# Queries x state in batches 0 to 3 by halves of TensorE's array, a second product for batch 1, a written order

## The chip, the core and the metric

The kernel runs on one core of a Trainium2 chip. The metric is the device time of one execution in microseconds (us), the median of the runs shown. Five engines work side by side, each with its own stream of instructions: PE (TensorE: matmuls, with PEld for its weight loads), DVE (VectorE), ACT (ScalarE), POOL (GpSimd) and SP (SyncE, which issues most transfers). They wait for each other by semaphores. SBUF is the working memory, PSUM (8 banks of 128 x 512 fp32) takes what PE writes.

## What is computed

Eight batches, eight heads, 576 positions, head size 64; linear attention with a norm, then a Fourier mixing and a feed-forward network (FFN):

```
kv  = einsum('bhsd,bhse->bhde', k, v)          # the state, 64 x 64 a head
out = einsum('bhsd,bhde->bhse', q, kv)         # queries x state
rms = sqrt(mean(out * out, axis=-1) + 1e-06)
x   = out / rms * g_norm                       # [8, 576, 512] after a transpose
u   = x + real(fft(fft(x, axis=1), axis=2))
un  = (u - mean(u)) / sqrt(var(u) + 1e-06)     # over the last axis
y   = u + relu(un @ w_ch1) @ w_ch2             # 512 -> 2048 -> 512
```

## The kernel before, in words

The attention, the Fourier mixing and a part of the FFN (the "early FFN", three of its sixteen slices of the hidden layer) are laid out as 1699 operations, each a Python closure that emits a handful of instructions of one engine. `Plan.run` (L443) lays them in an order: it walks through a time line with the costs that each operation was given, and on each engine takes the ready operation of the lowest rank whose buffers are free. The instructions emitted in the first 300 us of that time line are then tied to this order engine by engine (`pin`, L417). The ranks come from the batch and the stage (`rank`, L789), shifted by the table `SHIFT` (L55), one value for a stage, an engine and a rank, 275 in all. Behind the planned part the rest of the FFN follows (L1804 to L2338), most of it tied to the order in which it is written.

A batch goes through these stages. `plan_kv` (L919) forms the state on PE (L963, 64x64 quarters of the array) and copies it to SBUF on ACT (L988); for batch 0 DVE also writes a state scaled by g_norm (L998). `plan_q` (L1043) turns the queries on PE (L1055), and ACT copies them to `fq` (L1059). The 288 rows of a half of the sequence are three tiles of 96 rows (the first has 98), t = 0, 1, 2. `plan_out` (L1069) multiplies queries by state on PE (L1083), one PSUM bank for the even heads and one for the odd. A pair of heads lies on the partitions of one `fq` column block, 64 rows for each head; the weights are the queries, cut into 64 and 34 columns, so that each matmul uses one 64x64 quarter of the array: 2 sides x 4 pairs x 2 heads x 2 parts = 32 matmuls a product, which the trace shows as 64 records (each fp32 matmul here is two). Then ACT squares the product in PSUM (L1115), DVE sums the squares (L1120), and the product goes to `x`: in batch 0 a second product with the scaled state is made and ACT copies it (L1100); in batch 1 (`GAIN_AT_ONCE`) DVE copies it and multiplies by g_norm in one instruction (L1104); in batches 2 to 7 ACT copies it and POOL multiplies (L1133).

`plan_y` (L1140) makes 1/rms. `plan_fold` (L1176) multiplies `x` by it on DVE, one instruction a side (L1188), sums four columns for the zeroth frequency (L1193), and folds `x` (L1200). `plan_split` and `plan_folds` split it in two parts on POOL and ACT (L1217 to L1293), `plan_seq` (L1298, L1317) and `plan_chn` (L1352, L1361) are the two Fourier stages, and their result is added to `x` on DVE for batch 0 and on POOL for the others (L1400, L1403). `plan_turn` (L1434) turns `x` on PE (L1459) and splits it into `unTh` and `unTl`. When a block of 512 tokens is turned, `plan_early` (L1544) runs the early FFN on it (L735, L753). `plan_w` (L1481) converts the weights, mostly on DVE (L671 to L680, L700, L1509), for PE's means L694.

PE also gets fillers that compute nothing that is used (L809, `plan_spare`): 30 at once, 40 and 22 more when 12 and 38 us of the planned time have passed, ranked behind all other work of PE.

Of the kernel before, what the change touches and what calls it, by code (L numbers as in the profile page):

```python
# [9 lines left out]
F32 = mybir.dt.float32  # L10
# [4 lines left out]
ALU = mybir.AluOpType  # L15
# [12 lines left out]
NA = 3  # L28
# [26 lines left out]
SHIFT = {  # L55
    ("", "DVE", -100): -32718,
    ("", "DVE", 85): 3,
    ("", "HOST", 0): 2612.5,
    ("", "HOST", 9000): 2922.5,
    ("", "PE", 85): 147129,  # L60
    ("", "POOL", 20): 10887.5,
    ("", "POOL", 40): 273026.5,
    ("", "POOL", 50): 16174,
    ("", "POOL", 60): 1017789,
    ("", "POOL", 70): 281483.5,
    ("", "SP DMA", -40): -314778,
    ("", "SP DMA", 10): -20802,
    ("", "SP DMA", 20): 72028,
    ("", "SP DMA", 85): 2143.5,
    ("chn", "ACT", -34): 1891,  # L70
    ("chn", "ACT", 16): 4142,
    ("chn", "ACT", 26): 116005,
    ("chn", "ACT", 36): 50922.5,
    ("chn", "ACT", 46): -188.5,
    ("chn", "ACT", 56): 2260,
    ("chn", "ACT", 66): 110596,
    ("chn", "ACT", 76): 8930,
    ("chn", "DVE", -34): -62060.5,
    ("chn", "DVE", 16): 5303,
    ("chn", "DVE", 26): 368,  # L80
    ("chn", "DVE", 36): -19935,
    ("chn", "DVE", 46): -922,
    ("chn", "DVE", 56): -4020.5,
    ("chn", "DVE", 66): 21267,
    ("chn", "DVE", 76): -121.5,
    ("chn", "PE", -34): -28856,
    ("chn", "PE", 16): -65422,
    ("chn", "PE", 26): 521738.5,
    ("chn", "PE", 36): 17419.5,
    ("chn", "PE", 46): 5106,  # L90
    ("chn", "PE", 56): 518354.5,
    ("chn", "PE", 66): 62546,
    ("chn", "PE", 76): 6630.5,
    ("chn", "POOL", 16): 32868,
    ("chn", "POOL", 26): -43448,
    ("chn", "POOL", 36): -41076.5,
    ("chn", "POOL", 46): -6341.5,
    ("chn", "POOL", 56): -10643,
    ("chn", "POOL", 66): -356,
    ("chn", "POOL", 76): -2168,  # L100
    ("chn", "SP DMA", -34): -17259.5,
    ("chn", "SP DMA", 16): -1294,
    ("chn", "SP DMA", 26): -16518,
    ("chn", "SP DMA", 36): -290.5,
    ("chn", "SP DMA", 46): 17435,
    ("chn", "SP DMA", 56): 26457.5,
    ("chn", "SP DMA", 66): 16.5,
    ("chn", "SP DMA", 76): 7747,
    ("dft", "POOL", -37): 2039.5,
    ("dft", "SP DMA", -37): -192772.5,  # L110
    ("dft_d", "ACT", -35): 391,
    ("dft_d", "DVE", -35): -3433,
    ("dft_d", "POOL", -35): -9543.5,
    ("dft_d", "SP DMA", -35): -202629,
    ("dft_split", "ACT", -37): -41818.5,
    ("dft_split", "ACT", 9): 22267,
    ("dft_split", "POOL", -37): 19163,
    ("dft_split", "POOL", 9): -3864.5,
    ("early", "ACT", -100): -72646,
    ("early", "DVE", -100): 3540,  # L120
    ("early", "PE", 1000): 112,
    ("early", "PE", 1010): 57509,
    ("early", "PE", 1020): 41715.5,
    ("early", "PE", 1030): 133598,
    ("early", "PE", 1040): 42048.5,
    ("early", "PE", 1060): -1666,
    ("early", "PE", 1070): -100,
    ("early", "PE", 1080): 6247.5,
    ("early", "SP DMA", -100): 11271,
    ("fold", "DVE", -36): 29687.5,  # L130
    ("fold", "DVE", 14): 44762,
    ("fold", "DVE", 24): 13,
    ("fold", "DVE", 34): 4778,
    ("fold", "DVE", 44): 21,
    ("fold", "DVE", 54): -6924.5,
    ("fold", "DVE", 64): 4500,
    ("fold", "DVE", 74): -6233.5,
    ("folds", "ACT", 14): 10045,
    ("folds", "ACT", 24): -1988,
    ("folds", "ACT", 34): 110076,  # L140
    ("folds", "ACT", 44): 5822,
    ("folds", "ACT", 54): 23702.5,
    ("folds", "ACT", 64): -8652.5,
    ("folds", "ACT", 74): 1672,
    ("folds", "POOL", 14): 32875,
    ("folds", "POOL", 24): 8206,
    ("folds", "POOL", 34): 4127.5,
    ("folds", "POOL", 44): -47893.5,
    ("folds", "POOL", 54): 14868.5,
    ("folds", "POOL", 64): 7840,  # L150
    ("folds", "POOL", 74): 114,
    ("kv", "ACT DMA", -40): -329,
    ("kv", "ACT", -40): 1747,
    ("kv", "ACT", 10): -2622,
    ("kv", "ACT", 40): 1206,
    ("kv", "ACT", 50): 3461.5,
    ("kv", "ACT", 60): 6444.5,
    ("kv", "DVE", -40): -5070.5,
    ("kv", "PE", -40): -58409.5,
    ("kv", "PE", 10): -1672,  # L160
    ("kv", "PE", 20): -4880,
    ("kv", "PE", 30): -524.5,
# [12 lines left out]
    ("out", "ACT", -58): 1017.5,
# [2244 lines left out]
```

## Time and profile before

| | |
|---|---|
| median of 3 runs | 953.65 us (953.2 to 955.07) |
| profiled execution, its own time | 954.79 us |
| its span, first to last instruction | 953.0 us |
| busy in the span | PE 936.5, PEld 783.8, DVE 682.8, ACT 387.5, POOL 443.9 us |
| mean granted clock of PE | 0.998 of full speed |

The span is shorter than the time by what lies before the first and behind the last instruction, 1.8 us. Busy time of PE is the union of its matmuls, whose ends are modelled: a short gap between two small matmuls can hide in it, so the time that a product takes is read from where the next work starts. "Issue" as the end of an idle time means that the engine waited for nothing that the profile shows. The clock is given as a share of 2.4 GHz, at 0.50 it is 1.2 GHz.

### The profile page before, as it was taken

Reading aid. Unit: us, or ns where it says so; the run is one execution under the profiler, and the core shown is the slowest. Engines: PE = TensorE matmul, PEld = TensorE weight load, DVE = VectorE, ACT = ScalarE, POOL = GpSimd, SP = SyncE. Lnnn points to the kernel's source line nnn. Section 1 sums busy time; section 2 is a strip of 40 time slices with the busy share of each in tenths; the row PEclk is TensorE's granted clock in tenths of the full one; section 3 lists DMA queues with packets and bytes.
Section 4 is the critical chain, followed back from the end, with each engine's and each line's share of the span. In section 5 each row is a group of like instructions: output and inputs, shape, how many; then the busy total and the mean of one; then the engine's idle time right before and its main releaser. Section 6 shows DMA issues by size and latency. Waiting matters only on the chain.

```text
span 953.0 us, 18483 instructions
## 1 busy us (share of the span) xinstructions
PE 936.5 (98%) x7182; PEld 783.8 (82%) x7182; DVE 682.8 (72%) x1202; ACT 387.5 (41%) x743; POOL 443.9 (47%) x440
## 2 busy tenths in 40 slices
PE   9898999999999999999999999999999999999998
PEld 7787988888888877888888888888888888888886
DVE  5798787857948689999367876596658685674554
ACT  3666877778545323533314322342225212521110
POOL 3576787786644235656715053724462437210000
PEclk9999999999999999999999999999999999999999
DMA  8899587735456698988497496429543774213412
GB/s 271 229 288 313 163 285 233 255 98 195 166 204 247 235 384 325 371 300 291 176 379 304 146 341 253 173 76 332 200 154 111 254 280 181 81 76 140 182 55 88
DMA packets 108566, 210.53 MB, mean 221 GB/s; under 512 B 45292, under 2 KB 54400, under 8 KB 99520
## 3 DMA queue, kind: packets, MB, share of 16 engines
q1 hardware_dynamic: 105696, 199.92, 59.4%
q0 software_dynamic: 1920, 6.29, 1.8%
q10 hardware_dynamic: 864, 3.15, 1.0%
q8 instruction: 56, 0.92, 0.4%
q14 instruction: 30, 0.25, 0.1%
HBM read 141.40 MB, written 67.93 MB: 220 GB/s over the span
## 4 chain that ended last, share of the span: by engine, by line
PE 91%; DVE 3%; DMA 2%; ACT 2%; POOL 1%; issue 1%; DVEq 0%; SPq 0%; ACTq 0%; POOLq 0%
PE acc L2227 23%; PE ps_h L2192 20%; PE acc L1841 9%; PE ps_h L1830 9%; PE acc L753 8%; PE ps_h L735 8%; PE ps_f L1317 3%; PE ps_o L1083 3%; PE ps_s L809 2%; PE ps_f L1361 2%; PE ps_q L1055 2%; PE ps_t L1459 2%; PE ps_k L963 1%; DMA lp<-part_scr 1%; DMA unTh<-unT_scr 1%
## 5 line engine op out<-in xcount | busy, mean ns | idle before, releaser
L2227 PE MATMUL acc<-w2c,hh 128*128 128x512 f32 x640 | 197.6, 390 | 0.0
L745 ACT ACTIVATE hh<-ps_h 128x512 fp32r<-128x512 f32 x144 | 85.8, 597 | 220.7 <-PE ps_h L2192 90.0
L748 DVE SCALAR_TENSOR_TENSOR hl<-ps_h,hh 128x512 fp32r<-128x512 f32 x144 | 98.3, 687 | 90.5 <-ACT hh L745 90.2
L2227 PEld LDWEIGHTS acc<-w2c,hh 128*128 128x128 f32 x640 | 119.7, 188 | 25.5
L2237 DVE TENSOR_TENSOR us<-acc,us 128x512 f32<-128x512 f32 (+1 forms) x161 | 106.9, 681 | 43.0 <-PE acc L2227 42.6
L2227 PE MATMUL acc<-w2c,hl 128*128 128x512 f32 x320 | 124.5, 389 | 0.0
L2192 PE MATMUL ps_h<-t,w1c 128*128 128x512 f32 x480 | 115.3, 389 | 0.0
L2192 PEld LDWEIGHTS ps_h<-t,w1c 128*128 128x128 f32 x480 | 90.1, 188 | 18.7
L1863 POOL TENSOR_TENSOR us<-us,low 128x512 f32<-128x512 f32 x30 | 45.5, 1522 | 101.8 <-ACT low L1860 95.9
L2192 PE MATMUL ps_h<-b,w1c 128*128 128x512 f32 x360 | 91.2, 389 | 0.0
L2192 PEld LDWEIGHTS ps_h<-b,w1c 128*128 128x128 f32 x360 | 67.6, 188 | 14.0
L2227 PEld LDWEIGHTS acc<-w2c,hl 128*128 128x128 f32 x320 | 60.1, 188 | 12.4
L735 PE MATMUL ps_h<-unTh,w 128*128 128x512 f32 x216 | 67.5, 395 | 0.0
L753 PE MATMUL acc<-w,hh 128*128 128x512 f32 x216 | 67.3, 399 | 0.0
L1841 PE MATMUL acc<-w,hh 128*128 128x512 f32 x216 | 61.9, 390 | 0.0
L1830 PE MATMUL ps_h<-unTh,w 128*128 128x512 f32 x192 | 59.8, 392 | 1.0 <-DVE wa L1746 1.0
L2058 POOL TENSOR_TENSOR z<-z,low 128x512 f32<-128x512 f32 x24 | 30.9, 1296 | 60.7 <-DMA low<-unT_scr 60.5
L1133 POOL TENSOR_TENSOR x<-x,gb 96x512 f32<-96x512 f32 (+1 forms) x36 | 48.2, 1358 | 8.4 <-ACT x L1100 5.9
L2209 DVE TENSOR_TENSOR ps_h<-ps_h,s 128x512 f32<-128x512 f32 x60 | 39.8, 693 | 13.8 <-PE ps_h L2192 13.2
L2294 ACT COPY s<-ps_h 128x512 f32<-128x512 f32 x20 | 11.7, 587 | 92.8 <-PE ps_h L2192 92.8
L1841 PEld LDWEIGHTS acc<-w,hh 128*128 128x128 f32 x216 | 40.3, 188 | 8.6 <-DVE lp L1938 0.3
L735 PEld LDWEIGHTS ps_h<-unTh,w 128*128 128x128 f32 x216 | 39.7, 188 | 8.1
(208 smaller groups left out, 1939.5 us busy)
## 6 DMA issues: line engine op xcount, KB each, us to landing
w1c<-w_scr SPq DMA_DIRECT2D x13, 1792.0 KB, 9.9
raw<-in_moe_w_ch_dram SPq DMA_DIRECT2D x32, 512.0 KB, 4.0
w2c<-w_scr SPq DMA_DIRECT2D x14, 1024.0 KB, 5.1
unT_scr<-unTh SPq DMA_DIRECT2D x9, 1024.0 KB
unT_scr<-unTl SPq DMA_DIRECT2D x9, 1024.0 KB, 7.0
part_scr<-part SPq DMA_DIRECT2D x36, 256.0 KB, 2.7
w_scr<-w1q SPq DMA_DIRECT2D x5, 1792.0 KB
km<-in_k_dram SPq DMA_DIRECT2D x29, 288.0 KB, 5.8
```

What stands on the lines that cost most here:

```text
L735: nc.tensor.matmul(ps, w[c][:, kc * P : (kc + 1) * P], unT[a][:, kc, :], start=(idx == 0), stop=(idx == 3 * KC - 1),)
L745: nc.scalar.activation(hh, ps, AF.Relu)
L748: nc.vector.scalar_tensor_tensor(hl, ps, 0.0, hh.bitcast(F32), ALU.max, ALU.subtract)
L753: nc.tensor.matmul(acc, hpair[a][:, i * P : (i + 1) * P], w[c], start=(first and n == 0), stop=(last and n == 2),)
L1133: nc.gpsimd.tensor_tensor(v_, v_, gb[:n].unsqueeze(1).to_broadcast([n, H, D]), ALU.mult)
L1830: nc.tensor.matmul(ps, w1_of(f, c, kc), unTs[j][a][:, kc, :], start=(idx == 0), stop=(idx == 3 * KC - 1),)
L1841: nc.tensor.matmul(acc, hpair[a][:, i * P : (i + 1) * P], w2_of(f, c), start=(first_ and n == 0), stop=(last_ and n == 2),)
L1863: nc.gpsimd.tensor_tensor(ut, ut, part, ALU.add)
L2192: nc.tensor.matmul(ps, w[:, A_OF[m], c, kc * P : (kc + 1) * P], b[:, a, kc * BT : (kc + 1) * BT], start=(fresh and idx == 0), stop=(done a ...
L2209: nc.vector.tensor_tensor(to, a, b, ALU.add)
L2227: nc.tensor.matmul(ps, hpair[a][:, i * P : (i + 1) * P], w2c[n][:, r, c], start=(idx == 0), stop=(idx == 5),)
L2237: nc.vector.tensor_tensor(ut[:, cols], ps[:, cols], ut[:, cols], ALU.add)
```

## The change

`DOUBLE = (0, 1)`: batch 1 gets a scaled state and a second product as batch 0 has, and DVE's copy with g_norm (L1104) is gone; the ring of state tiles has three instead of two. `HALVES = (0, 1, 2, 3)`: in these batches the queries aren't cut any more, each matmul has all 98 (96) columns of weights and uses the 64 rows of one half of the array, 16 matmuls a product; batches 4 to 7 keep the quarters. The sums of squares are stored with the tile outermost, so that one DVE instruction scales both sides of a tile. The zeroth frequency's sum moves from DVE to POOL, as an addition of two columns each, and DVE adds the two results once at the end; the additions of the second Fourier stage now wait for it in the plan. The planner gets other costs for some loads, 1450 for a product by halves and 1040 for one by quarters. `SHIFT` is replaced by `ORDER`, a list of all operations for each engine; an operation's place in it becomes its rank, and the fillers stand in it among the other work. The numbers of the matmuls by quarters, of the fillers and of all transfers with their sizes stay as they are.

```diff
-SHIFT = {
-    ("", "DVE", -100): -32718,
...
-}
+ORDER = {
+    "DVE": (
+        1543, 1357, 1637, 1377, 1222, 1627, 1586, 1238, 1361, 1202, 1195, 1332, 1333, 1362, 610, 646, 1675,
...
+}
-GAIN_AT_ONCE = (1,)
+DOUBLE = (0, 1)
+HALVES = (0, 1, 2, 3)
...
-"kvt": 2
+"kvt": 3
...
-    def shift(self):
-        for o in self.ops:
-            stage = o.stage[len("plan_") :] if o.stage.startswith("plan_") else ""
-            o.rank += SHIFT.get((stage, o.eng + " DMA" * o.dma, round(o.rank)), 0)
+    def in_order(self):
+        for eng, order in ORDER.items():
+            for place, n in enumerate(order):
+                assert self.ops[n].eng == eng
+                self.ops[n].rank = place
...
+    x0p = cst.tile([P, 3, B, 2], F32, name="x0p")
...
-        if b:
+        if b not in DOUBLE:
             return kvt, kvt, [done], ld
...
-                293, rank(b, QT) + (2 - j if side else j) / 4,
+                245, rank(b, QT) + (2 - j if side else j) / 4,
...
+        parts = [slice(0, n)] if b in HALVES else [slice(0, D), slice(D, TR + 2)]
+        cost = 1450 if b in HALVES else 1040
...
-                        for part in (slice(0, D), slice(D, TR + 2)):
+                        for part in parts:
                             nc.tensor.matmul(
                                 pss[s].t[part, at : at + D],
                                 fqs[side].t[half, m, part],
...
-        a = g = op("PE", 1080, r, mm, done, [kvt, x, ss] + pss + fqs)
+        a = g = op("PE", cost, r, mm, done, [kvt, x, ss] + pss + fqs)
...
-            if fused:
-                c = op("DVE", 690, r - D1, og_gain, [g, i_gb], [psg[s], x])
-            else:
-                c = op("ACT", 590, r - D1, og, [g], [psg[s], x])
+            c = op("ACT", 590, r - D1, og, [g], [psg[s], x])
...
-        for s in range(2):
-            def mul(s=s):
-                v_ = xv(s).rearrange("p (h e) -> p h e", e=D)
-                y = yp.t[:n, : 6 * H].rearrange("p (s t h) -> p s t h", s=2, t=3)[:, s, t]
-                nc.vector.tensor_tensor(v_, v_, y.unsqueeze(2).to_broadcast([n, H, D]), ALU.mult)
-
-            ms.append(op("DVE", 690, r, mul, [y_done] + gs[s], [x, yp]))
+        def mul():
+            y = yp.t[:n, : 6 * H].rearrange("p (t g) -> p t g", t=3)[:, t]
+            x_ = x.t[:n].rearrange("p (h e) -> p h e", e=D)
+            nc.vector.tensor_tensor(
+                x_, x_, y.unsqueeze(2).to_broadcast([n, 2 * H, D]), ALU.mult
+            )
+
+        m = op("DVE", 1230, r, mul, [y_done] + gs[0] + gs[1], [x, yp])
...
-            nc.vector.tensor_reduce(x0[:n, t, b : b + 1], x.t[:n, :: DH], AX.X, ALU.add)
+            nc.gpsimd.tensor_tensor(x0p[:n, t, b], x.t[:n, :DM:DH], x.t[:n, DM::DH], ALU.add)
...
-        return f, op("DVE", 150, r, zero, ms + [i_x0], [x])
+        return f, op("POOL", 200, r, zero, [m, i_x0], [x])
...
-            adds = [op("DVE", 690, r, fn, pms, [x, pm], port=True) for fn in (add_l, add_r)]
+            adds = [op("DVE", 690, r, fn, pms + [zero], [x, pm], port=True) for fn in (add_l, add_r)]
...
     def p0_in():
+        nc.vector.tensor_tensor(x0, x0p[:, :, :, 0], x0p[:, :, :, 1], ALU.add)
```

## Rows read from the trace of the kernel before

**Rows 1.** The page, busy us (share of the span) xinstructions of each engine.

```profile
PE 936.5 (98%) x7182; PEld 783.8 (82%) x7182; DVE 682.8 (72%) x1202; ACT 387.5 (41%) x743; POOL 443.9 (47%) x440
```

**Rows 2.** Windows: length; busy us of PE, PEld, DVE, ACT, POOL; clock; DMA; GB/s.

```profile
11.36:87.25 75.89, 67.12 (x1740) 57.27 (x1739) 64.48 (x130) 49.94 (x113) 45.97 (x63) 0.98 0.89 263
87.25:150.00 62.75, 62.05 (x1005) 54.01 (x1008) 47.42 (x96) 46.95 (x106) 47.14 (x53) 1.00 0.80 252
150.00:300.00 150.00, 150.00 (x1559) 131.11 (x1550) 111.11 (x247) 95.18 (x206) 101.87 (x112) 1.00 0.52 181
300.00:375.00 75.00, 73.45 (x326) 59.56 (x325) 60.28 (x97) 25.89 (x46) 23.69 (x29) 1.00 0.87 314
```

**Rows 3.** Windows, shorter ones of the first stage, same columns.

```profile
26.00:36.00 10.00, 7.26 (x184) 6.10 (x175) 5.25 (x14) 3.93 (x9) 3.81 (x8) 1.00 1.01 283
36.00:50.00 14.00, 13.16 (x374) 10.71 (x373) 13.78 (x31) 12.35 (x30) 10.09 (x15) 1.00 0.73 193
...
60.00:75.00 15.00, 13.58 (x338) 11.90 (x336) 14.13 (x27) 11.64 (x28) 10.68 (x11) 1.00 0.88 304
```

**Rows 4.** Windows, L1083 alone: length; busy us of PE, PEld; clock; DMA; GB/s.

```profile
0.00:87.25 87.25, 17.38 (x768) 14.53 (x768) 0.98 0.89 269
87.25:150.00 62.75, 7.21 (x402) 6.38 (x406) 1.00 0.80 252
150.00:300.00 150.00, 10.11 (x572) 8.88 (x562) 1.00 0.52 181
```

**Rows 5.** Chain of waits to 400 us: start us, us, engine, tile, line, records.

```profile
126.84 1.08 PE ps_o L1083 x61
...
265.34 2.67 PE ps_f L1361 x24
```

**Rows 6.** Groups by line and shape, PEld: busy us, mean ns | idle.

```profile
L694 PEld LDWEIGHTS ps_w<-wp,mean_t 128*128 128x128 f32 x26 | 4.7, 188 | 1.4 <-POOL wp L690 0.5
...
L1659 PEld LDWEIGHTS ps_o<-cs,x0l 128*8 128x8 f32 x2 | 0.2, 88 | 0.1
```

**Rows 7.** Waits of PE, 11.36 to 87.25 us: total us, times, longest us.

```profile
PE ps_k L963 <- issue: 2.3, 2, 1.3
PE ps_t L1459 <- DVE wa L1509: 2.0, 1, 2.0
PE ps_o L1083 <- ACT kvt L988: 1.6, 2, 0.8
PE ps_o L1083 <- issue: 1.4, 1, 1.4
...
PE ps_k L963 <- ACT fq L1059: 0.2, 1, 0.2
```

**Rows 8.** Groups: DVE to 100 us, ACT, POOL to 300; columns as above.

```profile
L1104 DVE TENSOR_TENSOR x<-ps_o,gb 96x512 f32<-96x512 f32 (+1 forms) x6 | 3.8, 677 | 0.0
...
L998 DVE TENSOR_TENSOR kvt<-ps_k,gb 64x128 f32<-64x128 f32 x4 | 1.1, 286 | 0.1
...
L1100 ACT COPY x<-ps_o 96x512 f32<-96x512 f32 (+1 forms) x42 | 24.3, 586 | 8.6 <-PE ps_o L1083 8.2 <-DMA unT_scr<-unTl 0.2
...
L1601 POOL MEMSET ss<- 2x48 f32 x8 | 1.0, 133 | 0.4
...
L1162 POOL TENSOR_TENSOR rs_s<-rs_y,m 96x16 f32<-96x16 f32 x2 | 0.7, 360 | 2.8 <-DVE ps_y L1167 1.4 <-DVE rs_y L1158 1.3
```

**Rows 9.** Timeline of DVE: start us, us, line, operation, tiles, shapes, count.

```profile
39.60 1.27 DVE L1188 TENSOR_TENSOR x<-x,ps_y 96x512 f32<-96x512 f32 x2
40.91 0.15 DVE L1193 TENSOR_REDUCE x<-x 96x1 f32<-96x4 f32 x1
...
66.16 0.70 DVE L1400 TENSOR_TENSOR x<-x,pm 98x514 f32<-98x514 f32 x1
```

**Rows 10.** Windows around the stretch at half clock, columns as in rows 2.

```profile
75.50:78.88 3.38, 1.30 (x10) 0.94 (x11) 3.35 (x5) 1.65 (x6) 3.38 (x4) 1.00 1.02 246
78.88:82.29 3.41, 3.03 (x65) 2.62 (x67) 2.89 (x8) 2.81 (x6) 2.63 (x3) 0.50 0.80 234
```

More of the change, by code (lines that the diff above doesn't have):

```diff
@@ L334 @@
-GAIN_AT_ONCE = (1,)
+ORDER = {
+    "DVE": (
[21 rows of a table added]
+    ),
[13 rows of a table added]
+    ),
[21 rows of a table added]
+    ),
+    "TICK": (
+        35, 76,
+    ),
+    "ACT": (
[23 rows of a table added]
+    ),
+    "POOL": (
[13 rows of a table added]
+    ),
+    "HOST": (
+        1609, 1608, 1607,
+    ),
+}
+DOUBLE = (0, 1)
+HALVES = (0, 1, 2, 3)
 RINGS = {
-    "p8": 8, "part": 2, "unT": 2, "h": 2 * NA, "qt": 2, "fq": 4, "kvt": 2, "kv": 8, "kr": 2, "xst": 1, "x": 9, "raw": 2, "e2": 5, "wk": 2, "xhl": 3, "pt": 1, "two": 2, "far": 1,
+    "p8": 8, "part": 2, "unT": 2, "h": 2 * NA, "qt": 2, "fq": 4, "kvt": 3, "kv": 8, "kr": 2, "xst": 1, "x": 9, "raw": 2, "e2": 5, "wk": 2, "xhl": 3, "pt": 1, "two": 2, "far": 1,
@@ L795 @@
     D1, D2 = 20, 0
[L798 removed]
+    i_x0 = op("DVE", 60, URGENT, lambda: nc.vector.memset(x0p, 0.0))
     i_sgn = dma(9, rank(1, 0), lambda: nc.sync.dma_start(sgn_t, sign))
@@ L1126, in plan_out @@
             cs_.append(c)
-        if kvg is not kvt or fused:
+        if kvg is not kvt:
             return ds, [cs_, cs_]
@@ L1350, in plan_seq, with plan_chn @@
         ]
-    def plan_chn(b, t, x, pt, dones):
+    def plan_chn(b, t, x, pt, dones, zero):
         n = rows[t]
@@ L1407, in plan_chn @@
         if b == 0:
-            adds = [op("DVE", 690, r, fn, pms, [x, pm], port=True) for fn in (add_l, add_r)]
+            adds = [op("DVE", 690, r, fn, pms + [zero], [x, pm], port=True) for fn in (add_l, add_r)]
         else:
-            adds = [op("POOL", 1240, r, fn, pms, [x, pm]) for fn in (add_l, add_r)]
+            adds = [op("POOL", 1240, r, fn, pms + [zero], [x, pm]) for fn in (add_l, add_r)]
         r0 = b * S + 1
@@ L1491, in plan_w @@
         ps, pf = bank_buf("ps_a"), ring("wk", one, [P, DM], "wp")
-        a = dma(500 if which == 1 else 350, r if r_load is None else r_load, lambda: w_load(which, f, raw.t), after, [raw])
+        a = dma(442 if which == 1 else 385, r if r_load is None else r_load, lambda: w_load(which, f, raw.t), after, [raw])
         src = ring("wk", one, [P, DM], "wa") if which == 1 else ps
         late_ = f >= NA
+        pool_lo = late_ and which == 1
         high = ps if late_ else pf
@@ L1516, in lo @@
             h, l = w_t[which, f]
-            eng = nc.gpsimd if late_ and which == 1 else nc.vector
+            eng = nc.gpsimd if pool_lo else nc.vector
             eng.tensor_tensor(l, src.t, h.bitcast(F32), ALU.subtract)
@@ L1535, in plan_w @@
         g = op("ACT", 640, r, lambda: hi(src), [e], [src])
-        pool_lo = late_ and which == 1
         w_done[which, f] = op(
             "POOL" if pool_lo else "DVE", 1340 if pool_lo else 700, r, lambda: lo(src), [g], [src],
-            port=(which == 1),
+            port=(which == 1 and not pool_lo),
         )
@@ L1595 @@
         ss = Placed("two", lambda at: (
-            two.tile([P, 2, 3, H], F32, name="ss", tag=f"ss{at}"),
+            two.tile([P, 3, 2, H], F32, name="ss", tag=f"ss{at}"),
             *[two.tile([P, 6 * H], F32, name=c, tag=f"{c}{at}") for c in ("m", "rs_s", "rs_y")],
```

298 lines of the change are left out of this document (8 added, 290 removed), and 90 rows, old and new, of the table ORDER.

## Prediction

> **What bounds the kernel now.** I read the page's busy line first [rows 1]: PE is busy 936.5 of 953.0 us, so the kernel stands and falls with PE's work, and only 16.5 us of PE's idle time are there to be won. Then the windows, to see where they lie [rows 2]: 8.77 us from 11.36 to 87.25 us, 0.70 to 150 us, none to 300 us, 1.55 to 375 us, and the other 5.5 us at the start and behind 375 us. From 87.25 us, where the first matmul of the early FFN starts, PE runs without a gap to speak of: what is added to PE there is added to the time, and what other engines save there is worth nothing. Before 87.25 us ("the first stage") it is a chain through several engines. From 36 to 50 and from 60 to 75 us DVE has hardly a gap (13.78 busy of 14.00 us, 14.13 of 15.00) [rows 3]. The work of batches 0 to 2's queries x state lies in this stage, that of batch 3 behind it: 768 records of L1083 before 87.25 us are 12 products of 64, and 6 + 3 + 3 is batches 0, 1 and 2 [rows 4].
>
> **The change part by part.** The sum is made against the profiled execution, span 953.0 us and time 954.79 us; the median of the runs shown is 953.65 us. I add the difference of the spans to the median.
>
> *Halves, price of one product.* Before, 32 fp32 products of 64x64 quarters leave 64 records and take 1.08 us where nothing disturbs them [rows 5], 17 ns a record, or 68 ns in each quarter of the array. After, 16 products with 98 (96) columns of weights leave 32 records, 16 in each half. No row shows this form, so I bound it. Moving data are the same 64 columns. If these set the pace in a quarter, a record of a half takes 68 ns too, 16 of them 1.08 us: the lower end, no gain below it, since each half has to pass the 16 records in turn. The weight load grows: 8 columns take 88 ns, 128 take 188 ns [rows 6], that is 0.83 ns a column, 82 ns for 98 columns against 53 for 64. If the load sets the pace, and the 68 - 53 = 15 ns over it stay, it is 97 x 16 = 1.55 us: the upper end as long as the load runs beside the matmul before it. I take 1.45, close to the upper end, since the 64-column load is near the 68 ns measured and nothing else grows by the change but the load. (The planner is told 1450 in the diff; that is an input, not a measurement shown here.) The Trainium skill, TensorE: Matmul & The Clock Gate, section LDWEIGHTS (loading the stationary operand), says that a load takes its columns divided by 1.2 in ns, whatever the rows. The trace agrees (0.83 ns a column). By this rule fewer instructions are bought with a longer load, and the sum below would use the upper end: PE would need 73.3 us in the first stage instead of 71.8, which gives 952.4 us; by the lower end it would need 66.2, and DVE's gain alone stands, 950.1 us.
>
> *Batch 3, behind 87.25 us.* 3 x (1.45 - 1.08) = **+1.1 us** (0 to +1.4), all of it on the path, for PE has no gap there.
>
> *Batches 0 to 2, first stage.* There the quarters don't reach 1.08: the 12 products are 17.38 us of PE's busy time, 1.45 each [rows 4], stretched by short gaps between instructions and by a low clock. Behind 87.25 us the same form takes 17.32 us for 974 records, 1.14 a product. So 12 half products of 1.45 cost nothing more if the shorter stream loses the stretching, 12 x 0.1 = 1.2 more at 1.55, and 12 x 0.47 = 5.6 more if it keeps the 0.37 us as well. I take 0, because half as many instructions are to be supplied, and the only instructions of PE that wait for nothing but "issue" are these small ones, L963 for 2.3 us and L1083 for 1.4, inside the 8.77 us [rows 7].
>
> *Second product of batch 1.* Three more products: **+4.35 us** of PE (3.2 to 5.8 with stretching), in the first stage. It removes six L1104 on DVE (3.8 us) and adds four L998 (1.1 us): DVE **-2.7**. It adds six L1100 copies of 586 ns to ACT, +3.5 us [rows 8]. A third state tile is in the ring, and each tile of batch 1 holds four PSUM banks where it held two.
>
> *The scaling in one instruction, the zero on POOL.* Two L1188 (1.27 us together where they follow each other) become one of the same elements; only the start of the second can fall away, so at most 0.1 a tile, taken as 0. L1193 (0.15 us) leaves DVE [rows 9]: 6 tiles in the first stage, **-0.9**; the other 18 lie beside a full PE and are worth nothing. On POOL the small addition costs 0.13 to 0.36 us a tile by its smallest rows [rows 8]; POOL is busy 46 of 75.89 us in the stage and 101.87 of 150 behind it [rows 2], which covers it. Without that cover it would be 24 x 0.36 = 8.6 us. Batch 0's additions on DVE now wait for POOL's zero as well; queued behind them on DVE are the splits of the turned tiles, which PE's early FFN needs. But the zeros are due some 20 us before (L1193 of batch 0 ran up to 41 us, the additions from 66 us [rows 9]), so I cost the wait at 0; if POOL came to one of them last, the path would grow by that addition, 0.4 us at most. One more DVE instruction before the p0 matmuls lies beside a full PE: 0.
>
> *The written order.* Every operation gets a place of its own. The list is a set of ranks (the planner takes the first that is ready), so it doesn't show which gap closes. Its bounds: below, nothing of PE's idle time before 375 us is left, -11; above, it opens gaps in work that now has none. PE's fillers (L809, 92 of them, 62 behind 11.36 us) are no longer last in PE's list but stand among batches 0 to 3; their number is the same, so they add nothing to PE's sum, only may go first where useful work is ready. DMA issues on SP move in the same way; their data are unchanged. I take 0 for the order.
>
> *The sum.* DVE's chain in the first stage gets 2.7 + 0.9 = 3.6 us shorter: 75.9 - 3.6 = 72.3 us. PE's need in it: 67.12 - 17.38 = 49.7 of other work, 15 products x 1.45 = 21.8, waits on ACT (1.6 + 0.2) [rows 7], less the stretch at half clock. That is from 78.88 us, where the granted clock is 0.50 (1.2 GHz) for 3.41 us behind a stretch in which PE was busy 1.30 of 3.38 us [rows 10], waiting 2.0 us for DVE [rows 7]; the work there at 1.2 GHz would take about half the 3.03 us, 1.5 us less, at 2.4 GHz. 49.7 + 21.8 + 1.8 - 1.5 = 71.8, just under 72.3: DVE still ends the stage, PE is next. So 953.65 - 3.6 + 1.1 = **951.1 us**.
>
> **The rivals.**
> *B, the stage shrinks by more.* Halves pace like quarters (1.08) and the order also fills DVE's gaps before 36 us (5.25 busy of 10.00 from 26 to 36 us [rows 3]). PE then needs 49.7 + 16.2 + 1.8 - 1.5 = 66.2; the stage ends with DVE at about 68: -8, batch 3 at 0: 945.7. For it: the issue waits. Against: the load rows.
> *C, ACT takes DVE's place.* From 36 to 50 us ACT is busy 12.35 of 14.00 us [rows 3]; with 3.5 more it needs 15.9, so batch 1's copies and squares end later by up to 1.9 and DVE's 3.6 are not seen: 953.65 + 1.1 + (0 to 1.9) = 954.8 to 956.6. Against: batch 1's products may lie elsewhere in the new order.
> *D, slower: the half products make PE the bound of the first stage.* It decides from (72.3 - 49.7 - 1.8) / 15 = 1.39 us a product, without the clock's help. At 1.55 + 0.37 = 1.92 they take 28.8 us; with the idle time other than "issue" (8.77 - 3.7 = 5.1) the stage is 49.7 + 28.8 + 5.1 = 83.6, +7.7, and batch 3 +1.4: 962.7. A price between 1.45 and 1.92 gives 955 to 962.
> *E, a half doesn't load beside its matmul*, or the halves don't run side by side, so the change doesn't do what it says: 82 + 55 ns (64 of L1361's 130 columns at 111 ns [rows 5]) is 137 x 16 = 2.2 us. Stage 49.7 + 33 + 1.8 = 84.5, +8.6; batch 3 +3.4: 965.6. Against: in a quarter 53 + 55 = 108 would be more than the 68 measured. The Trainium skill, TensorEngine Tiling (Array Packing), sections Theoretical Speedup and When to Use Tiling, advises tiling of the columns too where the stationary side has up to 64, for up to twice the speed; giving it up could, as an estimate from that page, cost 2 x 1.08 = 2.16 a product, about the same result.
>
> **How the numbers follow.** Forecast A 0.31 (949.5 to 953), B 0.20 (943 to 949), C 0.25 (953 to 957), D 0.18 (957 to 963), E 0.06. Likeliest A: 951.1. Leaving out B's lower part (0.09) and E with D's top (0.10): 945.5 to 961. A measurement of this kernel can tell 0.2%, 1.9 us, from no change: faster is below 951.7, slower above 955.6. Faster is B and three quarters of A, 0.44; slower is D, E and two fifths of C, 0.34; the rest 0.22. A's own range is 949.5 to 953.
>
> **What would show it.** L1083 with 16 x 2 records a product: 1.45 us or 1.08 decides between A and B, 1.9 or 2.2 for D and E. The first matmul of L735: at 83 to 84 us in A, 79 in B, 87 or later in C, 94 in D. The clock stays at 1.00 around 79 us in A. "Issue" waits of L1083 shrink. ACT's window around batch 1 is full in C. The prediction is wrong if PE has gaps behind the first early FFN, or if the order moves other work into the first stage, so that its end no longer stands for the whole.

## The result and the profile after

| | before | after |
|---|---|---|
| median of the timed runs, us | 953.72 (953.2 to 955.57, 6 runs) | 969.61 (962.22 to 971.52, 6 runs) |
| ratio, with its 95% interval | | 1.0149 [1.0114, 1.0184] |
| profiled execution: time / span, us | 954.79 / 953.0 | 962.22 / 960.4 |
| second profile: time / span, us | | 972.25 / 970.5 |

The change made the kernel 1.5% slower, some 15 us, where 951.1 us (945.5 to 961) had been forecast. The first profile caught the shortest of the six runs: the others have spans of 964.6 to 969.7 us and a mean granted clock of 0.991 to 0.996 against its 0.998. So a second profile was taken (run a4 below), and the two are read side by side. In the changed file the products' line is L918 (L1083 before), kv's L796 (L963), the early FFN's first and second matmul L567 and L585 (L735 and L753), p0's matmuls L1486.

The busy line of the page, the counterpart of [rows 1], in the first profile of the changed kernel:

```profile
PE 945.7 (98%) x6798; PEld 793.0 (83%) x6798; DVE 675.8 (70%) x1153; ACT 391.7 (41%) x749; POOL 452.4 (47%) x464
```

The windows of [rows 2] in the same profile, with the columns as there:

```profile
11.36:87.25 75.89, 75.15 (x1498) 66.44 (x1500) 60.21 (x116) 52.92 (x121) 48.53 (x67) 1.00 0.95 272
87.25:150.00 62.75, 62.75 (x877) 54.91 (x870) 43.48 (x83) 46.19 (x101) 51.24 (x62) 1.00 0.81 257
150.00:300.00 150.00, 146.13 (x1528) 127.07 (x1528) 106.79 (x219) 96.28 (x208) 103.50 (x123) 0.99 0.51 173
300.00:375.00 75.00, 70.31 (x308) 56.64 (x308) 57.42 (x90) 25.33 (x45) 20.56 (x26) 1.00 0.78 286
```

and in the second profile, with one window more, a stretch at half clock:

```profile
11.36:87.25 75.89, 71.54 (x1386) 62.56 (x1378) 59.11 (x109) 49.10 (x112) 47.26 (x66) 0.98 0.92 260
87.25:150.00 62.75, 62.75 (x812) 55.57 (x815) 41.44 (x82) 40.84 (x90) 42.63 (x53) 0.91 0.77 241
...
84.92:98.57 13.65, 13.59 (x162) 12.39 (x163) 9.02 (x18) 7.23 (x15) 4.37 (x4) 0.50 0.84 271
```

Three things are to be seen. First, PE's idle time of 8.77 us in the first stage [rows 2] is all but gone in the first profile (75.89 - 75.15 = 0.74): what the change meant to do there happened. Second, behind 150 us idle time is new: 3.87 us to 300 us where there was none, 4.69 from there to 375 us where there were 1.55. Third, PE's busy time grew by 945.7 - 936.5 = 9.2 us, and by 15.6 in the second profile, where 13.65 us run at half the clock with PE busy all but 0.06 us of them.

The waits of PE from 11.36 to 420 us in the first profile (total us, times, longest us):

```profile
PE ps_o L1486 <- DVE x0h L1476: 3.8, 1, 3.8
PE acc L585 <- ACT hh L577: 1.9, 2, 1.2
PE ps_h L1657 <- ACT w L1340: 1.2, 1, 1.2
PE ps_h L1657 <- DVE wa L1573: 0.8, 1, 0.8
PE acc L1668 <- ACT hh L577: 0.7, 1, 0.7
PE ps_k L796 <- DMA vm<-in_v_dram: 0.4, 1, 0.4
PE ps_q L888 <- ACT x L935: 0.2, 1, 0.2
```

Unlike in [rows 7], no wait is put down to "issue" any more. The largest wait stands at 265 us, before p0's matmuls.

### The profile page after: what moved, and what is told of

It is laid out like the page before. It is cut to its first block, busy times and chain, and to the rows that moved or that the text cites. A ratio compares the mean times of both kernels' runs of the same rounds, so it can differ in the third digit from the quotient of the medians.

```text
span 960.4 us, 17686 instructions
## 1 busy us (share of the span) xinstructions
PE 945.7 (98%) x6798; PEld 793.0 (83%) x6798; DVE 675.8 (70%) x1153; ACT 391.7 (41%) x749; POOL 452.4 (47%) x464
## 4 chain that ended last, share of the span: by engine, by line
PE 63%; DMA 2%; DVE 1%; issue 0%; DVEq 0%; SPq 0%
PE acc L2054 23%; PE ps_h L2019 20%; PE acc L1668 10%; PE ps_h L1657 9%; DMA lu<-u_scr 1%; PE acc L585 1%; DMA raw<-in_moe_w_ch_dram 1%; PE ps_w L526 0%; DVE wp L512 0%; DVE bst L1706 0%; PE ps_t L1725 0%; DVE ps_a L496 0%; DVE wp L509 0%; DVE wa L1573 0%; DVE wa L532 0%
## 5 line engine op out<-in xcount | busy, mean ns | idle before, releaser
L585 PE MATMUL acc<-w,hh 128*128 128x512 f32 x216 | 69.0, 404 | 2.0 <-ACT hh L577 1.9
L567 PE MATMUL ps_h<-unTh,w 128*128 128x512 f32 x216 | 67.7, 394 | 0.0
L1668 PE MATMUL acc<-w,hh 128*128 128x512 f32 x216 | 62.3, 391 | 0.7 <-ACT hh L577 0.7
L2036 DVE TENSOR_TENSOR ps_h<-ps_h,s 128x512 f32<-128x512 f32 x60 | 39.8, 693 | 13.8 <-PE ps_h L2019 13.2
L585 PEld LDWEIGHTS acc<-w,hh 128*128 128x128 f32 x216 | 39.6, 191 | 10.5 <-ACT hh L577 2.8
L1668 PEld LDWEIGHTS acc<-w,hh 128*128 128x128 f32 x216 | 40.3, 188 | 9.4 <-ACT hh L577 1.1
```

What stands on the lines that cost most here:

```text
L567: nc.tensor.matmul(ps, w[c][:, kc * P : (kc + 1) * P], unT[a][:, kc, :], start=(idx == 0), stop=(idx == 3 * KC - 1),)
L585: nc.tensor.matmul(acc, hpair[a][:, i * P : (i + 1) * P], w[c], start=(first and n == 0), stop=(last and n == 2),)
L1668: nc.tensor.matmul(acc, hpair[a][:, i * P : (i + 1) * P], w2_of(f, c), start=(first_ and n == 0), stop=(last_ and n == 2),)
L2036: nc.vector.tensor_tensor(to, a, b, ALU.add)
```

## The experiments

Theory 1 comes from the first trace alone: the parts do as forecast, and the written order costs the time by new gaps behind 230 us. Theory 2 is that the parts themselves cost it. Theory 3 came from the first four runs: products by halves let the granted clock fall and stay low. In the runs "in the old order" every operation is issued at the place that it had in the kernel before (a few move by one or two places for want of a free bank), by a list in place of the planner's choice. The code cuts show the lines that matter, some of them shortened, without the lists of places; what stands behind # is a note. Those of a1, a2, a3, b3 and c1 are against the changed kernel, that of d1 is against c4, and the others are against the kernel before.

**a1: all parts, old order.**

```
-        self.in_order()                    # and the choice by time
+        todo = list(REPLAY)                # the order of the kernel before
```

> All parts of the change (halves for batches 0 to 3, second product of batch 1, scaling in one instruction, zero on POOL), but every operation issued at the place that it had in the kernel before; the second products of batch 1 stand right behind their first ones, and 12 operations move by one or two places for want of a free PSUM bank. Theory 1 (the written order costs the time: it moves work forward, and pays for it with new gaps behind 230 us): the sum of the prediction without its order, 951 us, 949.5 to 956. Theory 2 (the parts themselves cost it, the order does not): 962 us or more, as with the written order.

Measured: 974.18 us, 1.0178 [1.0134, 1.0221]. Theory 1 falls: without the new order the loss is not smaller. These are two windows at half clock, with the columns of [rows 2]:

```profile
48.32:65.39 17.07, 16.03 (x130) 14.15 (x127) 4.26 (x8) 7.09 (x15) 3.80 (x6) 0.50 0.61 187
...
85.87:102.94 17.07, 16.81 (x224) 15.72 (x226) 12.10 (x22) 11.31 (x23) 9.41 (x9) 0.50 0.87 261
```

That is 34 us at half clock, and a third stretch of 3.41 us begins at 376 us; the profile of the kernel before has 3.41 [rows 10]. The first begins amid batch 1's half products, the second 2.2 us after a half product of batch 2 starts.

**a4: the changed kernel again.**

> The changed kernel once more, for a second profile and for times on the same chip: 962 to 972 us. If the profile falls on one of the longer runs, it shows further stretches at half clock (3.4 us each, some 1.7 us lost by each), and in front of each a gap of PE; theory 1 expects them behind the gaps of 325 to 350 us or behind 265 us. The rival is that they lie elsewhere, where PE has no gap.

Measured: 970.25 us, 1.0152 [1.0125, 1.0180]; the profile is the second one above. Theory 1's place is missed: the long stretch lies in the first stage. PE's timeline in front of it and in it (start us, us, line, operation, tiles, shapes, count, idle before):

```profile
72.99 1.51 PE L796 MATMUL ps_k<-vm,km 64*64 64x64 f32 x72 [1.41 <-DMA vm<-in_v_dram]
...
83.78 0.39 PE L1285 MATMUL ps_t<-ident,x 96*128 96x96 f32 x2 [0.86 <-DVE x L1229]
84.98 2.30 PE L1285 MATMUL ps_t<-ident,x 96*128 96x96 f32 x12 [0.81 <-ACT unTh L1294]
87.21 2.93 PE L918 MATMUL ps_o<-kvt,fq 64*98 64x64 f32 x32
...
92.64 2.83 PE L918 MATMUL ps_o<-kvt,fq 64*96 64x64 f32 x32
95.40 2.20 PE L796 MATMUL ps_k<-vm,km 64*64 64x64 f32 x72
97.53 1.20 PE L567 MATMUL ps_h<-unTh,w 128*128 128x512 f32 x2
```

In the first profile the same DMA held PE for 0.4 us and the two waits of 0.8 are absent; there the clock stayed at 1.00. In these two profiles the longer run is thus the one with short waits ahead of a stretch that holds two half products; for the other runs no trace was kept.

**a3: quarters, new order.**

```
-HALVES = (0, 1, 2, 3)
+HALVES = ()
```

> The changed kernel with products by quarters again (32 instructions of TensorE's quarters a product, as before), the order and all else as changed. If a quarter product takes 1.08 us wherever PE is not short of other work, the 18 products of batches 0 to 3 save up to 18 x (1.5 - 1.08) = 7.6 us of PE, and PE is busy 74.9 of 75.64 us in the first stage, so that the time falls by 5 to 7.6 us. If the quarters take 1.45 us in the first stage for want of instructions, as in the kernel before, only batch 3 gains, 1.1 us, and waits put down to issue return: within 2 us of the changed kernel's.

Measured: 972.6 us, 1.0200 [1.0167, 1.0233]. There is no gain, so the first reckoning falls; the second (within 2 us) is missed by less than the noise, on the slower side. The same two waits of 0.8 us precede the same work, but with quarter products the clock is low there for only 3.41 us (another 3.41 us lie 14 us earlier, behind waits of 0.70 and 0.99 us):

```profile
92.17:95.58 3.41, 3.41 (x73) 3.29 (x64) 2.70 (x7) 2.06 (x6) 0.00 (x0) 0.50 0.93 315
```

What the quarters lose instead is seen in PE's waits from 11.36 to 100 us; the last line is the longest wait in the timeline:

```profile
PE ps_o L918 <- issue: 7.6, 5, 3.0
...
PE ps_k L796 <- issue: 1.0, 1, 1.0
...
53.08 0.46 PE L918 MATMUL ps_o<-kvt,fq 64*34 64x64 f32 x17 [3.01 <-issue]
```

In the new order batch 1's six products follow one another closely. As quarters they are stopped three times, for 4.8 us in all, and batch 0's twice, for 2.8; as halves they are not stopped. That they want for instructions fits the packed trace, which also times the transfers of the instruction queue (q8, 16 KB each): three ended at 46.52, 51.83 and 55.60 us, and PE went on at 47.98, 53.08 and 56.63. All nine "issue" waits of PE to 110 us, in this profile and in that of the kernel before, end 1.0 to 1.6 us behind the end of such a transfer. The gain of halves that the prediction hoped for in the "issue" waits is real, in the new order.

**b1: halves alone, in the kernel before.**

```
-                        for part in (slice(0, D), slice(D, TR + 2)):
+                        for part in ([slice(0, n)] if b < 4 else [slice(0, D), slice(D, TR + 2)]):
```

> The kernel before with one edit: the products of batches 0 to 3 by halves (32 instructions a tile), order and all else as before. The look back at the first four runs gave theory 3: where half products follow each other closely in the first stage, the granted clock falls to 0.50 and stays there (13.65 us in the second profile of the changed kernel, 17.07 us twice with the old order), while the same stall with quarter products cost 3.41 us. Theory 3: long stretches at 0.50 in the first stage, 13 to 34 us in all, time 958 to 972 us. Rival (a half product only costs its 1.45 us, as the prediction had it; the long stretches come from the second product and the order): 951 to 956 us, at most 3.4 us at 0.50.

Measured: 964.98 us, 1.0089 [1.0060, 1.0118]. Theory 3 holds, the rival falls.

```profile
48.67:55.49 6.82, 6.82 (x41) 5.93 (x40) 5.69 (x10) 4.08 (x9) 2.94 (x4) 0.50 0.89 279
...
75.97:93.04 17.07, 16.81 (x218) 15.60 (x219) 12.05 (x23) 11.42 (x23) 9.11 (x9) 0.50 0.93 273
```

With a third stretch of 3.41 us that is 27.3 us at half clock against 3.41. The sum of the gaps doesn't explain it: PE's waits from 11.36 to 93 us come to 2.6 us, less than before [rows 7].

```profile
PE ps_o L1083 <- ACT kvt L988: 1.2, 2, 0.9
PE ps_o L1083 <- DVE ss L1120: 1.1, 1, 1.1
PE ps_o L1083 <- DVE wa L700: 0.3, 1, 0.3
...
47.90 2.76 PE L1083 MATMUL ps_o<-kvt,fq 64*98 64x64 f32 x32 [1.05 <-DVE ss L1120]
73.92 2.31 PE L1083 MATMUL ps_o<-kvt,fq 64*96 64x64 f32 x32 [0.85 <-ACT kvt L988]
```

But each of the two long stretches begins 0.8 to 2.1 us behind a wait of 0.85 to 1.05 us, and it is much the same in a1. So what the halves are shown to change is how long the clock stays low; whether it would fall without such a wait was not tested. The work lost to the clock is at most (27.3 - 3.4) / 2 = 12 us, if it all takes twice as long there; the span is 10.7 us longer.

**c2: b1 with two wide matmuls ahead of each product.**

```
+                if b < 4 and not side:
+                    for ps in pss:      # 128x512, overwritten by the product
+                        nc.tensor.matmul(ps.t, still, wide, start=True, stop=True)   # wide: still, four times over
```

> The kernel before with halves for batches 0 to 3 (b1), and ahead of each of the 15 products two matmuls of 128x512 into the product's own two banks, which the product then overwrites: extra work of no use, 30 x 0.22 = 6.6 us of PE. Theory 3 (the half products let the clock fall because nothing wide runs among them for long): the 27 us at 0.50 of b1 shrink to some 3 to 7 us, which gives back 10 to 12 us against 6.6 spent: 957 to 961 us, less than b1's 965. Rival (half products lower the clock whatever runs between them, or the clock falls by gaps alone): 27 us at 0.50 stay, 968 to 972 us.

Measured: 963.08 us, 1.0077 [1.0046, 1.0109]. Of the 27.3 us at half clock one stretch of 10.24 us is left:

```profile
82.70:92.94 10.24, 9.89 (x140) 8.61 (x144) 6.35 (x13) 5.96 (x13) 5.65 (x6) 0.50 0.84 252
```

The work that is no use about paid for itself: 6.6 us were spent by the reckoning and (27.3 - 10.24) / 2 = 8.5 got back at most, and PE's busy time is 952.0 us in this profile against 952.4 in b1's; the intervals of the two times overlap. The rival (968 to 972) falls, though the total is 2 us above theory 3's range, as the stretch at the end of the stage stayed. What among the work lets the clock rise isn't settled: in a1, b1 and c2 the last stretch ended during 144 quarter records of kv, ahead of the first wide matmul, and the first stretch of a1 and b1 some 4 us into 14 wide ones.

**b4: halves for batch 3 alone.** The edit of b1 with `b == 3`.

> The kernel before with halves for batch 3 alone, whose three products stand behind 87 us between matmuls of 512 columns. The prediction's step: 3 x (1.45 - 1.08) = +1.1 us, 954 to 956, no stretch at 0.50 behind 87 us. Theory 3 expects the same, since the products stand apart and beside wide matmuls. Rival (each half product lowers the clock, wherever it stands): 3.4 us or more at 0.50 behind 87 us, +2.8 us or more.

Measured: 958.04 us, 1.0026 [1.0005, 1.0046], +2.5 us (0.5 to 4.4), and the clock is 1.00 from 87.25 to 150 us in its profile. The prediction's +1.1 lies in the interval; the rival's 3.4 us at half clock behind 87 us isn't there. Among matmuls of 512 columns these three half products did not lower the clock.

**b2: all parts but the halves, old order.** a1 with `HALVES = ()`.

> All parts of the change but the halves, in the old order: the run with the old order (973.4 us of span) with products by quarters again. Theory 3: the two stretches of 17.07 us at 0.50 shrink to 3.4 us each or less, span 973.4 - 13.7 or more, that is 952 to 960 us. Rival (the second product of batch 1 and the third state tile bring the low clock and the loss): 967 us or more.

Measured: 962.63 us, 1.0080 [1.0054, 1.0105]. Against a1 the two stretches of 17.07 us have shrunk to one of 6.83, as theory 3 has it, but the time lies 2.6 us above its range: something other than the halves costs 7 to 8 us.

**c4 and c3: the other two parts, each alone in the old order.**

```
-        if b:                              # c4: second product of batch 1
+        if b > 1:
-            ms.append(op("DVE", 690, r, mul, [y_done] + gs[s], [x, yp]))
+        m = op("DVE", 1230, r, mul, ...)   # c3: scaling in one, zero on POOL
```

> The kernel before, its order kept, with one part alone: batch 1's second product by quarters (three more products, each behind the first one), a third state tile, its copies on ACT. The prediction had DVE end the first stage, so that 2.7 us less of DVE and 4.35 us more of PE give 951 to 954 us. Rival (PE's own work and what it waits for on ACT end the stage, so that the three products and the six copies of ACT are seen): +3 to +8 us, 957 to 962.

> The kernel before, its order kept, with one part of the change alone: both halves of a tile scaled in one DVE instruction (at the place of the second), the zero position's sum as an addition on POOL, and p0's extra addition. The prediction's step: DVE 0.9 us shorter in the first stage, nothing else on the path: 952 to 955 us. Rival (POOL is late with its small additions, and the additions on DVE that wait for them hold PE's early FFN, or DVE's p0 copies are slowed): 957 us or more.

Measured: c4 962.01 us, 1.0076 [1.0051, 1.0101]; c3 955.15 us, 1.0011 [0.9991, 1.0031]. So the scaling and the zero cost nothing that can be told, as forecast, and the second product costs 7 us, as its rival had it. The three parts alone multiply to 1.0089 x 1.0076 x 1.0011 = 1.0177, and together (a1) they measured 1.0178. With intervals of 0.2 to 0.4% on each, so close a match is in part luck, but in sum the parts account for the loss in the old order. The windows of [rows 3] in c4:

```profile
36.00:50.00 14.00, 11.85 (x420) 9.75 (x409) 10.99 (x26) 10.83 (x26) 10.60 (x15) 1.00 0.73 194
50.00:60.00 10.00, 8.22 (x160) 7.07 (x160) 3.70 (x7) 6.16 (x13) 2.87 (x7) 1.00 0.72 246
```

DVE got its relief (10.99 busy where it had 13.78), and the stage grew all the same: the first wide matmul stands at 90.98 us instead of 87.18. No engine is full now. PE waits for ACT: each pair of products takes four banks, and the waits read as if the next pair couldn't start until ACT has copied.

```profile
PE ps_o L1046 <- ACT fq L1022: 1.1, 1, 1.1
PE ps_o L1046 <- ACT x L1063: 0.8, 2, 0.6
PE ps_q L1018 <- ACT x L1063: 0.7, 1, 0.7
...
PE ps_q L1018 <- ACT fq L1022: 0.6, 1, 0.6
```

The work from batch 1's first product to the group behind the fillers that follow its last one shows the whole loss (before, then c4):

```profile
42.45 2.12 PE L1083 MATMUL ps_o<-kvt,fq 64*64 64x64 f32 x64 [0.71 <-ACT kvt L988]
52.66 0.49 PE L1055 MATMUL ps_q<-ident,qt 96*128 96x96 f32 x4
...
41.30 3.10 PE L1046 MATMUL ps_o<-kvt,fq 64*64 64x64 f32 x128 [0.72 <-ACT kvt L951]
58.11 0.49 PE L1018 MATMUL ps_q<-ident,qt 96*128 96x96 f32 x4
```

It took 10.2 us and takes 16.8, that is 6.6 more: 3.2 us are the waits for ACT listed above, and 3.4 are the three products themselves (the products' busy time is 38.1 us in c4, 34.7 before).

**d1: c4 with batch 1's six copies on DVE.**

```
-                nc.scalar.copy(to, psg[s].t[:n].rearrange("p (u m d) -> p u m d", u=2, d=D))
+                eng = nc.vector.tensor_copy if b == 1 else nc.scalar.copy
+                eng(to, psg[s].t[:n].rearrange("p (u m d) -> p u m d", u=2, d=D))
```

> The second product alone (c4), with batch 1's six copies from PSUM on DVE instead of ACT; order and all else as in c4. Theory P (the three products themselves, 1.2 to 1.9 us each in a stage in which PE and what it waits for make one chain, cost the 7 us): within 2 us of c4's 962.0. Theory A (the six copies on ACT, 3.5 us in a stretch where ACT is 12.35 of 14 us busy in the kernel before, hold up the products that wait for ACT): 957 to 959.5 us, and PE's waits for ACT's x and fq (3.2 us in c4) shrink.

Measured: 960.05 us, 1.0044 [1.0018, 1.0069]; its interval overlaps c4's. Theory P holds, by a hair. In its profile PE waits for DVE's copies instead (L1064, 1.9 and 0.8 us), the same stretch takes 17.2 us (41.31 to 58.54), and ACT's split of the next batch (xhl) starts at 56.9 us, as in c4 (56.4; 51.0 before). So the engine of the copies isn't the cause of the stretch. That product and copy have to alternate is read from the waits; no run with more banks tested it. Whether the copies on ACT cost another 1 to 2 us stays open.

**d2: new order, one product for batch 1.** The changed kernel with `DOUBLE = (0,)` and the gain put on by DVE; some 45 operations around it move by a few places.

> The changed kernel in its written order with one part undone: batch 1 has one product again, and its gain is put on by DVE as before (some 45 operations around it move by a few places, since a freed bank or tile comes later or earlier). If the parts add up in the new order as in the old one (second product +7 us there), 962 to 964 us against the changed kernel's 969.6 and 970.3. Rival (the new order has found room for the second product): within 2 us of 970.

Measured: 967.91 us, 1.0135 [1.0101, 1.0169]: 2 us less than the changed kernel, within the intervals. In the new order the parts don't add up as in the old one: taking out the second product gains 2 us and taking out the halves (a3) none.

**a2, b3, c1: p0 at 265 us.** p0 is the computation for the zeroth frequency, which DVE prepares by small copies. These are DVE's timeline, then POOL's, in the first profile of the changed kernel:

```profile
264.64 0.71 DVE L1471 COPY x0t<-x 34x8 f32<-34x8 f32 x1
265.36 0.66 DVE L1473 COPY x0t<-x 32x8 f32<-32x8 f32 x1
266.04 1.21 DVE L1473 COPY x0t<-x 32x8 f32<-32x8 f32 x1
267.26 1.21 DVE L1475 COPY x<-x 32x8 f32<-32x8 f32 x1
...
264.60 1.41 POOL L1092 TENSOR_TENSOR xe<-ab 128x256 f32<-128x256 f32 x2 [0.77 <-DVE ab L1026]
265.96 2.49 POOL L1119 TENSOR_TENSOR xhl<-xe,xhl 128x512 fp32r<-128x512 f32 x2
```

A copy of eight columns takes 0.66 to 1.21 us and ends where a POOL instruction ends (267.25 and 267.23; 268.47 and 268.45); two of them with POOL at rest take 0.34 together (kernel before, 256.23 us). The Trainium skill, SBUF — State Buffer, section SBUF: two separate sides, says that DVE and GpSimd share a pair of ports as an exclusive lock: where a DVE instruction needs the pair, the one of the two that starts second is fully blocked. The trace agrees for these copies, each of which ends 0.02 us behind a POOL instruction.

```
-            nc.vector.tensor_copy(x0t[at : at + Q4], x0[2 * Q4 : TR, 0])    # a2: maxima, and p0_mm 1 us later
+            same(x0t[at : at + Q4], x0[2 * Q4 : TR, 0])                     # max(x, x)
+LATE, LATE_BY = (1393, 1394, 1395, 1396, 1397), 6000                        # b3: p0 6 us later, its result in a tile of its own
-        nc.vector.tensor_copy(x0h, x0[:, 1:])                               # c1: b3, p0_in on POOL
+        nc.gpsimd.tensor_copy(x0h, x0[:, 1:])
```

> The changed kernel with one place mended: p0's seven matmuls stand behind one more group of nine matmuls of the early FFN (1 us later in the plan; no other instruction changes place), and the five small copies ahead of them on DVE are written as maxima of a tile with itself, which give the same values. Theory 1 (PE's wait of 3.8 us at 265 us and the half clock behind it are two thirds of the loss): p0_in takes 9 x 0.17 = 1.6 us instead of 4.9 if the copies were slow because POOL was running, the wait and the half clock at 270 to 273 us go, span 960.4 - 3.8 - 1.7 = 955 us; if the runs of 966 to 971 us hang on the same stall, the median falls to 957. Rival (the time comes back at the next late input, ACT and DVE being behind anyway): the waits from 312 to 370 us grow by the same 4 to 5 us, and the time stays within 2 us of the changed kernel's. Rival for the copies: if they are slow whatever POOL does, the maxima also take 0.7 to 1 us each and a part of the wait stays.

> The changed kernel with p0's seven matmuls, their copies and three small DMAs issued 6 us later in the plan (PE: behind 13 groups of other matmuls; all other instructions keep their order; p0's result goes through a tile of its own). DVE's small copies stay as they were. Theory: the copies end when POOL's instruction beside them ends, so they still take some 5 us, but PE no longer waits for them: the 3.8 us at 265 to 280 us and the 3.41 us at 0.50 behind them go, -5.5 us against the changed kernel: 964 to 965 us in the median (970.25 and 969.61 measured), 955 to 957 in the best run. Rival (the time comes back at the next late input): within 2 us of the changed kernel's.

> The run with p0's matmuls later (b3), and p0's ten small preparing instructions issued on POOL instead of DVE. In b3 PE's wait did not go, it moved to the next thing that DVE makes (4.1 us for L1304), since DVE stood 4.9 us in the small copies, each of which ended when POOL's instruction beside it ended. Theory: on POOL the ten instructions wait for nobody, DVE goes on, and the wait of PE at 265 to 282 us and the half clock behind it go: 5.5 us less than the changed kernel, 964 to 965 in the median, 955 to 957 in the best run. Rival (POOL is then late with the even parts and low parts that PE needs next, some 10 x 0.2 = 2 us): a wait of 2 to 4 us in the same place, within 2 us of the changed kernel.

Measured: a2 966.75 us, 1.0133 [1.0105, 1.0162]; b3 970.49, 1.0142 [1.0100, 1.0184]; c1 965.06, 1.0109 [1.0071, 1.0147]. In a2 the maxima wait for POOL like the copies (2.64 us for three), 1.6 us of the wait stay and 1.4 us come back at L1304, and theory 1's 955 to 957 is missed. In b3 nothing is won, the rival is right: DVE stands still as long, and PE waits for its next output.

```profile
PE ps_f L1194 <- DVE unTl L1304: 4.1, 1, 4.1
```

In c1 the same instructions take 2.6 us on POOL in all, and that wait shrinks to 0.7; 2.1 us of PE's idle time are left to 300 us, and no stretch at half clock lies in its profile. In medians 5 us were won, as expected, but the intervals overlap. Its best run, 961.29, missed the 955 to 957. These windows of c1 show the change without any loss by clock:

```profile
11.36:87.25 75.89, 72.33 (x1378) 63.59 (x1371) 59.92 (x114) 51.01 (x117) 47.22 (x66) 1.00 0.94 267
...
300.00:375.00 75.00, 70.82 (x310) 57.12 (x309) 58.29 (x90) 25.01 (x44) 21.48 (x26) 1.00 0.78 289
```

Its span is 959.5 us and PE's busy time 944.2, which is 7.7 us over before; 7.1 of them are the products.

## Why the prediction was wrong

*The half product: right.* 1.45 us was taken. Behind 87 us a product starts 1.50 us before the next instruction (99.53 to 101.03 us), and two in a row take 2.94 us (41.03 us). That is 1.47 to 1.50 us, or some 92 ns a record in each half, near the upper end of 97. The rule of the Trainium skill (TensorE: Matmul & The Clock Gate, section LDWEIGHTS (loading the stationary operand)) by which the sum was to use that end fits: 82 of the 92 ns are its load, as an estimate by the columns. The longest load of L918 shown is 163 ns, which lies on the line of [rows 6] (88 + 90 x 0.83).

```profile
99.53 1.57 PE L918 MATMUL ps_o<-kvt,fq 64*96 64x64 f32 x32
101.03 1.21 PE L888 MATMUL ps_q<-ident,qt 96*128 96x96 f32 x12
...
L1083 PE MATMUL ps_o<-kvt,fq 64*34 64x64 f32 (+1 forms) x1728 | 34.7, 223 | 3.5 <-ACT kvt L988 1.6 <-issue 1.4 <-DVE wa L700 0.4
L918 PE MATMUL ps_o<-kvt,fq 64*64 64x64 f32 (+3 forms) x1344 | 41.8, 232 | 0.1
```

*Batch 3, +1.1: not contradicted* (b4). *The products' sum: nearly right.* Their busy time grew by 41.8 - 34.7 = 7.1 us (the groups by line above, all batches, before and after), where 5.45 had been reckoned.

*The clock: wrong in sign.* "Less the stretch at half clock, 1.5 us" took the clock as something that improves once PE waits less. The stretch of [rows 10] is gone in the first profile, so the marker "stays at 1.00 around 79 us" came true. But the step that puts batches 0 to 2 at 0 looked at each product's duration, and not at what a stage full of them does to the clock of everything else: +8.5 us for the halves alone (b1), with PE busy 16.81 of 17.07 us at 0.50. Rival D (962.7) named the half products and comes near b1's time, but by luck: its price was 1.92 us a product, where nearly all took 1.6 from first start to last end at full clock.

*DVE ends the stage: wrong.* This is the step on which the -3.6 us hung. DVE was busy 13.78 of 14 us [rows 3], and from that I read that it sets the stage's end. In the changed kernel's first profile DVE is down from 64.48 to 60.21 us between 11.36 and 87.25, and PE is busy 75.15 of these 75.89 us: PE's own work fills the stage. Its need had been put at 71.8 us. Measured to 87.25 us, the 15 products took 23.20 us where 21.8 had been reckoned, and the other work 75.15 - 23.20 = 51.95 where 49.7 had been. In the old order c4 shows it with one part alone: DVE's busy time fell by 2.5 us (682.8 to 680.3), and batch 1's stretch grew by 6.6. There the stage is a chain of product, copy, product; the four banks that a tile of batch 1 holds were named in the prediction and given no price (3.2 us of waits), and the 4.35 us of PE that had been laid beside DVE (3.4 as quarters in c4) were on the path.

*The order at 0: right as a net, by luck.* New against old order is 1.0149 and 1.0152 against 1.0178, with overlapping intervals. Inside, by the first profile, the new order took 8.0 us of PE's idle time from the first stage and 0.7 up to 150 us, and opened 7.0 behind: 3.8 of it for p0, whose DVE copies cost 4.9 us beside POOL where the kernel before paid 2.1, the rest late inputs of ACT and DVE from 312 us. The p0 step had been costed as "beside a full PE: 0", without asking what PE's new order puts right behind it. The bound "opens gaps in work that now has none" was in the text, and gaps behind the early FFN were named as a sign of being wrong; they had no size, and so didn't reach the range.

*The sum.* For the first profile PE's busy time is 9.2 us up and its idle time 1.8 down, together the 7.4 us by which the span grew. For the second PE's busy time is 15.6 us up (7.1 products; at most (13.65 + 3.41 - 3.41) / 2 = 6.8 clock; 1.7 unexplained) and its idle time 1.9, together 17.5. The marker "first matmul of L735 at 83 to 84 us" (now L567, at 87.99 and 97.53 us) couldn't tell alone: the order moves other work ahead of it (kv's records up to 87.25 us are 750 instead of 720), as the prediction's last sentence had feared.

The second profile isn't typical, though. Each run lists its span and its mean granted clock, and span x (1 - clock) estimates what half clock cost at most (13.8 us in b1's profile, where half of the 27.3 us is 13.7). The means, in us:

| | runs | span | half clock, at most | the rest |
|---|---|---|---|---|
| kernel before, beside the experiments | 46 | 953.4 | 4.1 | 949.3 |
| b1, halves alone | 5 | 962.1 | 10.2 | 951.9 |
| c4, second product alone | 6 | 960.8 | 4.3 | 956.5 |
| a1, all parts, old order | 4 | 970.9 | 15.5 | 955.4 |
| the changed kernel, with a4 | 10 | 967.3 | 6.0 | 961.3 |

By this estimate the clock makes up most of what the halves cost alone (6 of 9 us) and of what all parts cost in the old order (11 of 17.5), but only some 2 of the changed kernel's 14 us. The other 12 lie in PE's longer sum and in the new gaps. The two orders thus lose alike in sum and differently in kind. Nor do the kinds of a1 follow from b1 and c4, which together give 6 by the clock and 10 of the rest, where a1 has 11 and 6. What share of the 12 us each part has in the new order stays open, since taking out the halves (a3) or the second product (d2) gained nothing that can be told.

No run here beats the kernel before by more than can be told; c3 and it are alike.

## What to carry to other kernels

An engine that is 98% busy in a stage of a chain isn't shown to end it: take a microsecond off it first, or follow who waits for whom, and give every buffer that a step holds longer a price. Fewer instructions of a slower kind change more than their own time: look what granted clock the work around them then gets, and judge a tuned stage by several runs, since a wait of 1 us may decide whether 13 us go at half clock. Use the mean clock of all runs to tell how much of a loss is the clock's before explaining it by one profile. Moving a consumer behind a late producer helps only if the producer's engine isn't itself stuck: b3 won nothing; c1, which also took the work off the stuck engine, won 5 us in medians, with overlapping intervals.

## What the runs showed of the hardware that I had not expected

The granted clock was 0.50 for 17.07 us with PE busy 16.81 of them (b1) and rose again within a kind of work, not at the end of a gap. Eight-column DVE copies took 0.66 to 1.21 us, each to the end of the POOL instruction beside it, and two-input maxima no less. Quarter products that follow one another closely were stopped for up to 3.0 us and went on 1.0 to 1.6 us behind the end of a 16 KB instruction transfer (a3); half products were not stopped.
